# Attention beside an MLP on one core: score banks shared by all, the norm's small steps on GpSimd, and a table of order rules

## The chip, the cores and the metric

The kernel runs on one NeuronCore of a Trainium2 chip. Its engines work side by side, each on an instruction stream of its own, in order: TensorE (PE; its weight loads are PEld), VectorE (DVE), ScalarE (ACT), GpSimd (POOL) and SyncE (SP, which only issues DMAs). Streams wait for each other by semaphores. The metric is the device time of one execution in microseconds (us).

## What is computed

S = 2048 rows of D = 640, H = 32 query heads of width 20 that share one key and one value head, and an MLP of width F = 1536; all data are bfloat16.

```python
xn = (x - mean(x)) / sqrt(var(x) + 1e-5)
q = (xn @ wq) split into 32 heads;  k = xn @ wk;  v = xn @ wv
p = softmax(q @ k.T * 20 ** -0.5)          # per head, 2048 x 2048
A = concat_heads(p @ v) @ wo
B = square(relu(xn @ w1 + b1)) @ w2 + b2
out = x + A + B
```

## The kernel before

**Tiles and blocks.** A score tile has 128 keys by 512 queries of one head, one PSUM bank (PSUM has eight, `ps[:, 0:8]`). A block is one chunk of 512 queries (`QC` = 4) and four heads (`HPG`), so there are 32 blocks (`NBLK`) of 16 key tiles (`KT`) by four heads: 2048 score tiles in all. Each tile goes through one of two ways.

- *By ScalarE.* A step (`make_step`, `build_step`) takes two or three tiles; TensorE writes them with one group of matmuls, each on 20 of its rows (L320, `ps<-qT,kT`), and ScalarE turns them into exponentials with one activation (`make_act`, L864, `PT<-ps`). `PT` is a ring of 20 tiles (`PTR`). When the four heads of a key tile are there, a group of four matmuls on 32 columns each multiplies them with the values (`make_pv`, the PV sum, L320 `ps<-PT,vx`).
- *By VectorE.* Four tiles make a set (`new_set`, `make_dqk`). VectorE makes a linear function of each score whose 16-bit integer is the bit pattern of a coarse exponential (L1066, `D1`, `tmore<-ps`). Three passes over the set (L1084, `P1` to `P3`) add integers to it, and four weighted PV groups (`make_dpv`, `NTERM` = 4) make the sum smooth. A pass runs on GpSimd or on VectorE, chosen by the planned load of the two.

The PV groups of a block add up in one PSUM bank; a row of ones beside the values gives the softmax's denominator. VectorE copies the bank out (`TN`, L957), DMAs and small steps normalise it, and later units multiply it with `wo`.

**Units.** All other TensorE work is cut into units that are put between the steps: the transposes, keys, values and queries, the MLP's first matmul (`FFN`), its second alone (`FP`) or together with the attention's output (`OUT`). Each takes one PSUM bank, which VectorE empties. The last chunk's output is made after the last scores (the tail).

**Who sets the order.** A planner in the kernel's Python builds all streams before anything runs: a loop that holds a planned time for each engine and commits, each time, the operation that can start first, with a priority among those that could start within `EPS` of it. `par(name)` gives the planner's weights. Its table `RULES` can replace weights in single stages, where a stage is 10 us (`STG`) of planned ScalarE time; before, the table is empty. Where TensorE would stand idle too long, the planner puts in groups of four matmuls on zeros (`fill_parts`, L320, `ps<-kT,zeros`). A score group uses TensorE in another shape than the rest, for which the planner counts `SWITCH` at each change.

**Banks before.** `STATIC = True`: ScalarE's steps take banks 0, 1, 2 and banks 3, 4 in turn (`SIDES`), so three tiles and two tiles in turn. VectorE's tiles and the units share the remaining banks 5 to 7, of which the PV sum holds one; at the end of a block the next sum takes another of the three (`bank_for`, `pv_begin`), and `kept` keeps that one free for it. `DV` and the code behind it could let two steps of two tiles follow each other at once, but only without `STATIC`.

**The norm's small steps.** The rows are normalised in 16 parts (`rows(st)`). For most, VectorE makes the statistics (L379 to L381), adds epsilon to the variance (`VE`, L382) and, where the last step is GpSimd's (`POOLXN`), negates the mean (`NM`, L385); GpSimd raises the variance to the power -1/2 (`PW`, L387), and VectorE or GpSimd writes the normalised rows (`XN`, L389). `HOLD` lets loads start when a named operation is planned; that of `b2` hangs on `VE8`. VectorE passes that read and write SBUF alone and GpSimd's passes are marked `lock`, and the planner keeps them apart in its planned time.

The lines of the free choice of banks, which stood in the code before but did not run:

```python
t0 = max(free["PE"], horizon() - par("JIT"))
...
ok = [bk for bk in range(NB) if st_of[bk] is not None and st_of[bk] <= t0 + 0.02]
banks = None
if len(ok) >= 3 + par("R3"):
    ...                            # three adjacent banks of those
if banks is None:
    ...                            # the two adjacent banks that come free first
```

`horizon()` is the planned time at which ScalarE has done all steps so far; `JIT` is 0.8 us and `R3` is 2 by default.

Of the kernel before, what the change touches and what calls it, by code (L numbers as in the profile page):

```python
# [35 lines left out]
def _pl(z):  # L36
# [8 lines left out]
PTR = 20  # L45
NB = 8
PV0 = 7
SHARED = (4, 5, 6)
STATIC = True
SIDES = ((0, 1, 2), (3, 4))  # L50
POOLED = tuple(range(NB))
# [29 lines left out]
DJIT = 9.0  # L81
DV = 9
D1P = 1
RULES = {}
HOOK = None
# [26 lines left out]
DEFAULTS = dict(EVP=EVP, PBIAS=PBIAS, MPRIO=MPRIO, DGAP=DGAP, DLAST=DLAST, DRATE=DRATE, BEHIND=BEHIND, IDLE=IDLE, URG=URG, NOPEN=NOPEN,  # L112
                EPS=0.03, JIT=JIT, R3=R3, STATIC=STATIC, PVA=1, PVD=1, D1P=D1P, PP=4, SQP=2, DQP=3, QKP=0, ND=2, WARM=WARM, KEEP=KEEP, DJIT=DJIT, DV=DV)

# [63 lines left out]
def bass_parallel_sum__grouped_kv_mqa__dense_activation_squared_relu__prompt_kernel(nc, A_x, A_wq, A_wk, A_wv, A_wo, B_x, B_w1, B_b1, B_w2, B_b2, out):  # L178
    es = ExitStack()
    with es:  # L180
# [187 lines left out]
        def rows(st):  # L368

            p = ROWP[st // 4]  # L370
            if st in ACTST:
                k = ACTST.index(st)
                jk = OC[:, 0, :, :].rearrange("p c n -> p (c n)")[:, k * D:(k + 1) * D] if k < 4 else out_sb[:, k - 4, :]
                s1 = op(f"S{st}a", "ACT", 0.72, lambda e: e.activation(out=jk, in_=x_sb[:, st, :], func=AF.Identity, scale=-1.0 / D, accum_out=mv[:, st, 0:1]), [x_op[st]], lat=0.2)  # L374
                ag = op(f"S{st}b", "ACT", 0.9, lambda e: e.activation(out=jk, in_=x_sb[:, st, :], func=AF.Square, bias=mv[:, st, 0:1], accum_out=mv[:, st, 1:2]), [s1], lat=0.25)
                ve = op(f"VE{st}", "DVE", 0.08, lambda e: e.tensor_scalar(out=mv[:, st, 1:2], in0=mv[:, st, 1:2], scalar1=1.0 / D, scalar2=EPS, op0=ALU.mult, op1=ALU.add), [ag], prio=p - 0.1)
                opm = ALU.add
            else:
                s1 = op(f"S{st}a", "DVE", 0.40, lambda e: e.bn_stats(out=stats6[:, st, 0, :], in_=x_sb[:, st, 0:320]), [x_op[st]], prio=p)  # L379
                s2 = op(f"S{st}b", "DVE", 0.40, lambda e: e.bn_stats(out=stats6[:, st, 1, :], in_=x_sb[:, st, 320:640]), [x_op[st]], prio=p)  # L380
                ag = op(f"AG{st}", "DVE", 0.19, lambda e: e.bn_aggr(out=mv[:, st, :], in_=stats6[:, st, :, :].rearrange("p a b -> p (a b)")), [s1, s2], prio=p - 0.1)  # L381
                ve = op(f"VE{st}", "DVE", 0.08, lambda e: e.tensor_scalar(out=mv[:, st, 1:2], in0=mv[:, st, 1:2], scalar1=EPS, scalar2=None, op0=ALU.add), [ag], prio=p - 0.1)  # L382
                opm = ALU.subtract
                if st in POOLXN:
                    s1 = op(f"NM{st}", "DVE", 0.08, lambda e: e.tensor_scalar(out=mv[:, st, 0:1], in0=mv[:, st, 0:1], scalar1=-1.0, scalar2=None, op0=ALU.mult), [ag], prio=p - 0.1)  # L385
                    opm = ALU.add
# [72 lines left out]
        def fill_parts():  # L459
            return [mm(ps[32 * jj:32 * jj + 32, pv_bank[pv_blk[0]], :], zeros32[:, :], kT[:, 0:512], False, False, (0, 32 * jj)) for jj in range(4)]  # L460

        def warm_parts():
            return [lambda e: e.matmul(ps[:, PV0, :], ones_bf[:, :], hT_tmp[:, 0, :], start=True, stop=True)]  # L463

# [337 lines left out]
        def make_step():  # L802
# [7 lines left out]
            t0 = max(free["PE"], horizon() - par("JIT"))  # L810
            keep = kept()
            st_of = {bk: bank_state(bk) if bk != keep else None for bk in range(NB)}
            ok = [bk for bk in range(NB) if st_of[bk] is not None and st_of[bk] <= t0 + 0.02]
# [61 lines left out]

        pv_bank = {0: PV0}
        bank_busy[PV0] = True

        def bank_for(b):

            if b in pv_bank:
                return pv_bank[b]
            can = [(bank_state(bk), -bk) for bk in range(NB) if bank_state(bk) is not None and not (par("STATIC") and bk in HELD)]
            return -min(can)[1] if can else None

        def kept():

            b = pv_blk[0]
            return bank_for(b) if b < NBLK and b not in pv_begun else None

        def pv_begin(b):
            if b not in pv_begun:
                pv_bank[b] = bank_for(b)
                bank_busy[pv_bank[b]] = True
                pv_begun.add(b)

        def make_pv(b, kt):
            first, last = b not in pv_begun, pv_count[b] == KT - 1
            parts, deps = [], []
            bank = bank_for(b)  # L900
            for h in range(HPG):
                o, sl = tile_act[(b, kt, h)]
                deps.append(o)
                parts.append(mm(ps[32 * h:32 * h + 32, bank, :], vx[:, kt, :], PT[:, sl, :], first, last, (0, 32 * h)))
            deps.append(v_op[kt // 4])
            if first:
                deps.append(bank_rel[bank])
            return Op(f"PV{b}_{kt}", "PE", 0.222, parts, deps)

        def make_dpv(s, term):  # L910
# [4 lines left out]
            parts = []  # L915
            bank = bank_for(b)
            for h in range(HPG):
                i = s["order"].index(h)
                parts.append(mm(ps[32 * h:32 * h + 32, bank, :], wgt[:, kt, :], src[:, i * 512:(i + 1) * 512], first, last, (0, 32 * h)))
            deps.append(v_op[kt // 4])  # L920
            if term:
                deps.append(vs_op[kt // 4][term - 1])
            if first:
                deps.append(bank_rel[bank])
            return Op(f"DPV{b}_{kt}_{term}", "PE", 0.2205, parts, deps)
# [14 lines left out]
        def emit_norm(b, lastpv):  # L940
            marg = DMARG if b < NBLK - 3 else DMEND
            qc, g = divmod(b, G)
            a = b % NOR
            pb = pv_bank[b]
            if b >= NBLK - 2:
                Tn, T2 = OR[:, a, :], QCr[:, 0, :]
                tn = op(f"TN{b}", "DVE", 0.63, lambda e: e.transpose(out=Tn, in_=ps[:, pb, :]), [lastpv] + or_users[a], prio=0)
                tn.frees = pb
                rc = op(f"RC{b}", "DVE", 0.155, lambda e: e.reciprocal(out=Tn[:, DH:512:32], in_=Tn[:, DH:512:32]), [tn], prio=0)
# [6 lines left out]
                return  # L956
            tn = op(f"TN{b}", "DVE", 0.60, lambda e: e.tensor_copy(out=OR[:, a, :], in_=ps[:, pb, :]), [lastpv] + or_users[a], prio=0)  # L957
            tn.frees = pb
            tn_op[b] = tn
# [61 lines left out]
        def pool_banks():  # L1021

            keep = kept()
            if par("STATIC"):
                return [bk for bk in POOLED if bk not in HELD and bk != keep and bank_state(bk) is not None]
            fb = [bk for bk in POOLED if bk != keep and bank_state(bk) is not None]
            return fb if len(fb) > par("KEEP") else []
# [72 lines left out]
        def tail_bank():  # L1100
            done = not peek_tiles(1)[0]
            bs = [bk for bk in range(NB) if (bk not in HELD or done) and bank_state(bk) is not None]
            return min(bs, key=lambda bk: (bank_state(bk), bk)) if bs else None

# [67 lines left out]
        while True:  # L1172
# [36 lines left out]
            b = pv_blk[0]  # L1209
            if b < NBLK and (b == 0 or b - 1 in tn_op) and bank_for(b) is not None:  # L1210
                for k, (kind, x) in enumerate(pv_ready[b]):
# [75 lines left out]
            elif kind == "qk":  # L1287
                take_step(ap[1])
                heads = [t[2] for t in ap[1]["tiles"]]
                if len(heads) == 2 and not par("STATIC") and sum(1 for bk in POOLED if bank_state(bk) is not None and bank_state(bk) <= o.start + 0.06) >= par("DV"):  # L1290
                    can = [bk for bk in range(NB - 1) if all(k != kept() and bank_state(k) is not None and bank_state(k) <= o.start + 0.06 for k in (bk, bk + 1))]
                    st_ = build_step(len(steps), [can[0], can[0] + 1], 0.0) if can else None
                    if st_ is not None and len(st_["tiles"]) == 2 and not set(t[2] for t in st_["tiles"]) & set(heads):
                        rd = st_["qk"].ready()
                        if rd is not None and rd <= o.start + 0.06:
                            st_["qk"].dur = 0.005
                            commit(st_["qk"])
                            st_["qk"].lat = 0.425
                            take_step(st_)
                            heads += [t[2] for t in st_["tiles"]]  # L1300
                while len(heads) < HPG:
# [13 lines left out]
            elif kind == "pv":  # L1315
                pv_begin(ap[1])
                pv_of[(ap[1], pv_ready[ap[1]].pop(ap[2])[1])] = o
                finish_pv(ap[1], o)
            elif kind == "dpv":
                pv_begin(ap[1])  # L1320
                s_, term = ap[3], ap[4]
# [128 lines left out]
```

## Time and profile before

| | |
|---|---|
| median of 3 runs (lowest to highest) | 753.14 us (753.05 to 753.17) |
| profiled execution: time, span | 753.17 us, 751.4 us |
| granted TensorE clock | 0.999 |
| busy: TensorE, weight loads, VectorE, ScalarE, GpSimd | 716.6, 241.2, 580.0, 733.5, 292.0 us |
| exp activations (L864) | 640 |
| VectorE's score tiles (L1066) | 448 |
| passes (L1084): VectorE, GpSimd | 199, 137 |
| fills on zeros (`ps<-kT,zeros`) | 936 matmuls |

The span is from the first to the last instruction. Matmuls are pipelined and their ends are modelled, so a busy TensorE is not TensorE at its peak. An instruction's duration can overlap the next one's on the same engine. A releaser behind an arrow is what ended an idle time or a wait. L320 is a helper's line for most matmuls, so that the names of the tiles tell what they are.

### The profile page before, as it was taken

The page shows a single profiled execution, that of the slowest core. Times are in us where ns is not written, and L with a number is a line of the kernel's source. Part 1 is how long each engine was busy: PE and PEld are TensorE (multiplying, and loading weights), DVE is VectorE, ACT ScalarE, POOL GpSimd, SP SyncE. Part 2 cuts the span into 40 slices and gives each one's busy share as a digit, 9 for nine tenths or more (in the row PEclk, how much of TensorE's full clock was granted, in tenths as well). Part 3 has the DMA queues.
Part 4 walks back from the last instruction along what each step waited for, and adds up shares of the span by engine and source line. Part 5 has one row for each costly group of instructions (what it writes and reads, how often), then busy time and mean ns, then how long its engine had stood idle before and what let it go on. Part 6 is the DMA issues. An engine that isn't in the chain of part 4 may idle for free.

```text
span 751.4 us, 23326 instructions
## 1 busy us (share of the span) xinstructions
PE 716.6 (95%) x10359; PEld 241.2 (32%) x10361; DVE 580.0 (77%) x990; ACT 733.5 (98%) x662; POOL 292.0 (39%) x195
## 2 busy tenths in 40 slices
PE   8999998999999999999999999999999999999997
PEld 4432223333222333332222333332222233332223
DVE  7768887786887868969887878778887875777882
ACT  6899999999999999999999999999999999999995
POOL 3714534343553424314135522332434542337452
PEclk9999999999999999999999999999999999999999
DMA  5327232316841111121000111101102111110001
GB/s 188 109 60 195 72 105 66 114 46 141 191 93 28 26 41 45 38 55 27 21 15 16 33 49 51 43 24 35 25 21 90 44 31 56 35 30 20 22 10 37
DMA packets 42017, 44.05 MB, mean 59 GB/s; under 512 B 15540, under 2 KB 32772, under 8 KB 41788
## 3 DMA queue, kind: packets, MB, share of 16 engines
q1 hardware_dynamic: 39132, 36.93, 17.8%
q0 software_dynamic: 2208, 5.25, 3.6%
q8 instruction: 81, 1.33, 0.7%
q10 hardware_dynamic: 576, 0.38, 0.2%
q14 instruction: 20, 0.16, 0.1%
HBM read 28.03 MB, written 14.91 MB: 57 GB/s over the span
## 4 chain that ended last, share of the span: by engine, by line
ACT 94%; PE 4%; DMA 1%; DVE 1%; SPq 0%; issue 0%; DVEq 0%
ACT PT L864 94%; PE ps L320 3%; DMA x_sb<-in_A_x_dram 1%; PE ps L463 0%; PE ps L493 0%; DVE out_sb L1144 0%; PE ps L521 0%; PE ps L449 0%; ACT OC L374 0%; SPq L337 0%; DVE OR L379 0%; DVE kT L507 0%; PE ps L428 0%; SPq L344 0%; ACT xnT L430 0%
## 5 line engine op out<-in xcount | busy, mean ns | idle before, releaser
L864 ACT ACTIVATE PT<-ps 128x1536 bf16<-128x1536 f32 (+1 forms) x640 | 723.8, 1424 | 6.4 <-PE ps L320 6.3
L1066 DVE TENSOR_SCALAR tmore<-ps 128x512 uint16<-128x512 f32 x448 | 299.5, 686 | 112.3 <-PE ps L320 109.7
L320 PE MATMUL ps<-qT,kT 20*128 20x512 bf16 x2048 | 267.9, 384 | 27.7 <-ACT PT L864 24.8
L1084 POOL TENSOR_SCALAR tmore<-tmore 128x2048 uint16<-128x2048 uint16 x81 | 153.4, 1898 | 242.4 <-DVE x_sb L1084 85.8
L1084 POOL TENSOR_SCALAR x_sb<-tmore 128x2048 uint16<-128x2048 uint16 x56 | 106.4, 1902 | 169.6 <-DVE x_sb L1084 114.5
L320 PEld LDWEIGHTS ps<-qT,kT 20*128 20x128 bf16 x2048 | 66.8, 91 | 281.3 <-ACT PT L864 270.9
L320 PE MATMUL ps<-PT,vx 128*32 128x512 bf16 x1600 | 152.9, 387 | 0.6 <-DVE OR L957 0.5
L1084 DVE TENSOR_SCALAR x_sb<-tmore 128x2048 uint16<-128x2048 uint16 x129 | 92.6, 743 | 0.9
L320 PE MATMUL ps<-kT,zeros 128*32 128x512 bf16 x936 | 74.9, 381 | 0.0
L320 PE MATMUL ps<-xnT,w_sb 128*32 128x512 bf16 x960 | 71.0, 382 | 0.0
L320 PE MATMUL ps<-w_sb,big 128*32 128x320 bf16 x1536 | 70.4, 301 | 0.0
L320 PE MATMUL ps<-x_sb,vxs 128*32 128x512 bf16 x740 | 65.9, 382 | 0.2
L320 PEld LDWEIGHTS ps<-PT,vx 128*32 128x32 bf16 x1600 | 39.8, 93 | 74.8 <-issue 68.0
L320 PE MATMUL ps<-tmore,vxs 128*32 128x512 bf16 x604 | 52.3, 381 | 0.0
L1084 DVE TENSOR_SCALAR tmore<-tmore 128x2048 uint16<-128x2048 uint16 x70 | 51.6, 754 | 0.4
L320 PE MATMUL ps<-tmore,vx 128*32 128x512 bf16 x448 | 43.8, 381 | 0.2 <-DVE QCr L565 0.2
L601 DVE TENSOR_SCALAR hT_tmp<-ps,b1col 128x512 bf16<-128x512 f32 x48 | 35.8, 747 | 10.4 <-PE ps L320 10.0
L320 PEld LDWEIGHTS ps<-w_sb,big 128*32 128x32 bf16 x1536 | 34.7, 96 | 25.6 <-issue 16.1
L320 PE MATMUL ps<-xnT,wq_sb 128*32 128x512 bf16 (+1 forms) x480 | 30.8, 355 | 0.0
L320 PE MATMUL ps<-wo_c,OC 128*32 128x320 bf16 x608 | 29.1, 301 | 0.0
L320 PEld LDWEIGHTS ps<-kT,zeros 128*32 128x32 bf16 x936 | 21.7, 95 | 21.7 <-issue 12.6
L320 PEld LDWEIGHTS ps<-xnT,w_sb 128*32 128x32 bf16 x960 | 20.5, 95 | 25.2 <-issue 13.6
(82 smaller groups left out, 300.2 us busy)
## 6 DMA issues: line engine op xcount, KB each, us to landing
xbd<-b2d SPq DMA_DIRECT2D x16, 320.0 KB, 4.4
xbd<-in_A_x_dram POOLq DMA_DIRECT2D x8, 640.0 KB, 6.2
xr<-xbd SPq DMA_DIRECT2D x32, 160.0 KB, 2.4
w_sb<-in_B_w_dram SPq DMA_DIRECT2D x8, 480.0 KB, 5.0
big<-OR SPq DMA_DIRECT2D x71, 40.0 KB
big<-drs SPq DMA_DIRECT2D x71, 40.0 KB
out_dram<-out_sb SPq DMA_DIRECT2D x15, 160.0 KB, 1.8
qT<-QCr SPq DMA_DIRECT2D x108, 20.0 KB
```

The source lines that it names most:

```text
L320: return lambda e: e.matmul(out_, l, r, start=start, stop=stop, tile_position=tp)
L601: o = Op(f"RL{qc}_{f}", "DVE", 0.66, [lambda e: e.tensor_scalar(out=hT_tmp[:, k % 2, :], in0=ps[:, bk, :], scalar1=b1col[:, f:f + 1], scal ...
L864: return Op(f"ACT{st_['j']}", "ACT", 0.05 + 0.4267 * n, [lambda e: e.activation(out=PT[:, s0:s0 + n, :], in_=ps[:, b0:b0 + (n - 1) * db + ...
L1066: d1 = op(f"D1_{n}_{i}", "DVE", 0.60, lambda e: e.tensor_scalar(out=L[:, cs].bitcast(U16), in0=ps[:, bank, :], scalar1=XA, scalar2=XB, op0 ...
L1084: p = op(f"P{j}_{n}", eng, 0.60 if eng == "DVE" else 1.86, lambda e, T=T, j=j, two=two: e.tensor_scalar(out=T.bitcast(U16), in0=L.bitcast( ...
```

## The change

- `STATIC = False`: a step takes its banks from seven (`NB`), 0 to 6, by the rule quoted above; VectorE's tiles and the units take theirs from the same seven (`pool_banks`).
- The PV sum stays in bank 7 (`PVB`). The first PV group of a block waits for the copy `TN` of the block before. `kept`, `bank_for` and `pv_begin` go, and so does the second score step of `DV`.
- In the row parts from the fifth on, `VE` (without ScalarE's statistics) and `NM` are GpSimd's, with other priorities.
- `RULES` gets entries for most of the stages 1 to 69.
- The tail may use bank 7 once the last block's copy is planned.

The core of the diff, with the table of rules cut to a few of its lines:

```diff
 PTR = 20
-NB = 8
-PV0 = 7
+NB = 7
+PVB = 7
 SHARED = (4, 5, 6)
-STATIC = True
-SIDES = ((0, 1, 2), (3, 4))
+STATIC = False
+SIDES = ((0, 1), (2, 3))
 POOLED = tuple(range(NB))
...
 DJIT = 9.0
-DV = 9
-D1P = 1
-RULES = {}
+RULES = {1: {'PVA': 0.95, 'EPS': 0.2, 'DGAP': 0.8},
...
+         3: {'JIT': 0.9, 'R3': 0},
...
+         12: {'R3': 2, 'ND': 1, 'JIT': 1.0, 'MPRIO': 1.1},
...
+         15: {'R3': 1},
...
+         30: {'NOPEN': 3, 'DQP': 2.05, 'EPS': 0.12},
+         38: {'DQP': 2.05, 'PBIAS': 2.5},
...
+         52: {'DGAP': 1.5, 'MPRIO': 0.9, 'BEHIND': 0.5, 'PBIAS': 2.5, 'R3': 1, 'NOPEN': 2, 'D1P': 1, 'DRATE': 1.1, 'DLAST': 3.5, 'EVP': 2, 'EPS': 0.06, 'PP': 4, 'SQP': 0.7, 'URG': 4},
...
+         67: {'R3': 9, 'WARM': 0.78, 'NOPEN': 1, 'URG': 2, 'D1P': 1, 'ND': 2, 'MPRIO': 0.9, 'DQP': 0.95},
...
+         69: {'R3': 0, 'WARM': 0.78, 'NOPEN': 1, 'URG': 2, 'D1P': 0.5, 'ND': 2, 'MPRIO': 0.9, 'DQP': 0.95, 'PBIAS': 1}}
 HOOK = None
 DEFAULTS = dict(EVP=EVP, PBIAS=PBIAS, MPRIO=MPRIO, DGAP=DGAP, DLAST=DLAST, DRATE=DRATE, BEHIND=BEHIND, IDLE=IDLE, URG=URG, NOPEN=NOPEN,
-                EPS=0.03, JIT=JIT, R3=R3, STATIC=STATIC, PVA=1, PVD=1, D1P=D1P, PP=4, SQP=2, DQP=3, QKP=0, ND=2, WARM=WARM, KEEP=KEEP, DJIT=DJIT, DV=DV)
+                EPS=0.03, JIT=JIT, R3=R3, STATIC=STATIC, PVA=1, PVD=1, D1P=1, PP=4, SQP=2, DQP=3, QKP=0, ND=2, WARM=WARM, KEEP=KEEP, DJIT=DJIT)
...
             p = ROWP[st // 4]
+            small, pp = (("DVE", 0.08), p - 0.1) if st < 4 else (("POOL", 0.13), st // 4 - 0.5)
             if st in ACTST:
...
                 ag = op(f"AG{st}", "DVE", 0.19, lambda e: e.bn_aggr(out=mv[:, st, :], in_=stats6[:, st, :, :].rearrange("p a b -> p (a b)")), [s1, s2], prio=p - 0.1)
-                ve = op(f"VE{st}", "DVE", 0.08, lambda e: e.tensor_scalar(out=mv[:, st, 1:2], in0=mv[:, st, 1:2], scalar1=EPS, scalar2=None, op0=ALU.add), [ag], prio=p - 0.1)
+                ve = op(f"VE{st}", *small, lambda e: e.tensor_scalar(out=mv[:, st, 1:2], in0=mv[:, st, 1:2], scalar1=EPS, scalar2=None, op0=ALU.add), [ag], prio=pp)
                 opm = ALU.subtract
                 if st in POOLXN:
-                    s1 = op(f"NM{st}", "DVE", 0.08, lambda e: e.tensor_scalar(out=mv[:, st, 0:1], in0=mv[:, st, 0:1], scalar1=-1.0, scalar2=None, op0=ALU.mult), [ag], prio=p - 0.1)
+                    s1 = op(f"NM{st}", *small, lambda e: e.tensor_scalar(out=mv[:, st, 0:1], in0=mv[:, st, 0:1], scalar1=-1.0, scalar2=None, op0=ALU.mult), [ag], prio=pp)
                     opm = ALU.add
...
         def fill_parts():
-            return [mm(ps[32 * jj:32 * jj + 32, pv_bank[pv_blk[0]], :], zeros32[:, :], kT[:, 0:512], False, False, (0, 32 * jj)) for jj in range(4)]
+            return [mm(ps[32 * jj:32 * jj + 32, PVB, :], zeros32[:, :], kT[:, 0:512], False, False, (0, 32 * jj)) for jj in range(4)]
...
         def warm_parts():
-            return [lambda e: e.matmul(ps[:, PV0, :], ones_bf[:, :], hT_tmp[:, 0, :], start=True, stop=True)]
+            return [lambda e: e.matmul(ps[:, PVB, :], ones_bf[:, :], hT_tmp[:, 0, :], start=True, stop=True)]
...
             t0 = max(free["PE"], horizon() - par("JIT"))
-            keep = kept()
-            st_of = {bk: bank_state(bk) if bk != keep else None for bk in range(NB)}
+            st_of = {bk: bank_state(bk) for bk in range(NB)}
             ok = [bk for bk in range(NB) if st_of[bk] is not None and st_of[bk] <= t0 + 0.02]
...
-        pv_bank = {0: PV0}
-        bank_busy[PV0] = True
-
-        def bank_for(b):
-
-            if b in pv_bank:
-                return pv_bank[b]
-            can = [(bank_state(bk), -bk) for bk in range(NB) if bank_state(bk) is not None and not (par("STATIC") and bk in HELD)]
-            return -min(can)[1] if can else None
-
-        def kept():
-
-            b = pv_blk[0]
-            return bank_for(b) if b < NBLK and b not in pv_begun else None
-
-        def pv_begin(b):
-            if b not in pv_begun:
-                pv_bank[b] = bank_for(b)
-                bank_busy[pv_bank[b]] = True
-                pv_begun.add(b)
-
         def make_pv(b, kt):
...
             parts, deps = [], []
-            bank = bank_for(b)
             for h in range(HPG):
...
                 deps.append(o)
-                parts.append(mm(ps[32 * h:32 * h + 32, bank, :], vx[:, kt, :], PT[:, sl, :], first, last, (0, 32 * h)))
+                parts.append(mm(ps[32 * h:32 * h + 32, PVB, :], vx[:, kt, :], PT[:, sl, :], first, last, (0, 32 * h)))
             deps.append(v_op[kt // 4])
-            if first:
-                deps.append(bank_rel[bank])
+            if first and b > 0:
+                deps.append(tn_op[b - 1])
             return Op(f"PV{b}_{kt}", "PE", 0.222, parts, deps)
...
             parts = []
-            bank = bank_for(b)
             for h in range(HPG):
                 i = s["order"].index(h)
-                parts.append(mm(ps[32 * h:32 * h + 32, bank, :], wgt[:, kt, :], src[:, i * 512:(i + 1) * 512], first, last, (0, 32 * h)))
+                parts.append(mm(ps[32 * h:32 * h + 32, PVB, :], wgt[:, kt, :], src[:, i * 512:(i + 1) * 512], first, last, (0, 32 * h)))
             deps.append(v_op[kt // 4])
...
                 deps.append(vs_op[kt // 4][term - 1])
-            if first:
-                deps.append(bank_rel[bank])
+            if first and b > 0:
+                deps.append(tn_op[b - 1])
             return Op(f"DPV{b}_{kt}_{term}", "PE", 0.2205, parts, deps)
...
             a = b % NOR
-            pb = pv_bank[b]
             if b >= NBLK - 2:
                 Tn, T2 = OR[:, a, :], QCr[:, 0, :]
-                tn = op(f"TN{b}", "DVE", 0.63, lambda e: e.transpose(out=Tn, in_=ps[:, pb, :]), [lastpv] + or_users[a], prio=0)
-                tn.frees = pb
+                tn = op(f"TN{b}", "DVE", 0.63, lambda e: e.transpose(out=Tn, in_=ps[:, PVB, :]), [lastpv] + or_users[a], prio=0)
                 rc = op(f"RC{b}", "DVE", 0.155, lambda e: e.reciprocal(out=Tn[:, DH:512:32], in_=Tn[:, DH:512:32]), [tn], prio=0)
...
                 return
-            tn = op(f"TN{b}", "DVE", 0.60, lambda e: e.tensor_copy(out=OR[:, a, :], in_=ps[:, pb, :]), [lastpv] + or_users[a], prio=0)
-            tn.frees = pb
+            tn = op(f"TN{b}", "DVE", 0.60, lambda e: e.tensor_copy(out=OR[:, a, :], in_=ps[:, PVB, :]), [lastpv] + or_users[a], prio=0)
             tn_op[b] = tn
...
-            keep = kept()
             if par("STATIC"):
-                return [bk for bk in POOLED if bk not in HELD and bk != keep and bank_state(bk) is not None]
-            fb = [bk for bk in POOLED if bk != keep and bank_state(bk) is not None]
+                return [bk for bk in POOLED if bk not in HELD and bank_state(bk) is not None]
+            fb = [bk for bk in POOLED if bank_state(bk) is not None]
             return fb if len(fb) > par("KEEP") else []
...
             bs = [bk for bk in range(NB) if (bk not in HELD or done) and bank_state(bk) is not None]
+            if tn_op.get(NBLK - 1) is not None and tn_op[NBLK - 1].fin is not None and not bank_busy[PVB]:
+                bank_rel[PVB] = bank_rel[PVB] or tn_op[NBLK - 1]
+                bs.append(PVB)
             return min(bs, key=lambda bk: (bank_state(bk), bk)) if bs else None
...
             b = pv_blk[0]
-            if b < NBLK and (b == 0 or b - 1 in tn_op) and bank_for(b) is not None:
+            if b < NBLK and (b == 0 or b - 1 in tn_op):
                 for k, (kind, x) in enumerate(pv_ready[b]):
...
                 heads = [t[2] for t in ap[1]["tiles"]]
-                if len(heads) == 2 and not par("STATIC") and sum(1 for bk in POOLED if bank_state(bk) is not None and bank_state(bk) <= o.start + 0.06) >= par("DV"):
-                    can = [bk for bk in range(NB - 1) if all(k != kept() and bank_state(k) is not None and bank_state(k) <= o.start + 0.06 for k in (bk, bk + 1))]
-                    st_ = build_step(len(steps), [can[0], can[0] + 1], 0.0) if can else None
-                    if st_ is not None and len(st_["tiles"]) == 2 and not set(t[2] for t in st_["tiles"]) & set(heads):
-                        rd = st_["qk"].ready()
-                        if rd is not None and rd <= o.start + 0.06:
-                            st_["qk"].dur = 0.005
-                            commit(st_["qk"])
-                            st_["qk"].lat = 0.425
-                            take_step(st_)
-                            heads += [t[2] for t in st_["tiles"]]
                 while len(heads) < HPG:
...
             elif kind == "pv":
-                pv_begin(ap[1])
+                pv_begun.add(ap[1])
                 pv_of[(ap[1], pv_ready[ap[1]].pop(ap[2])[1])] = o
...
             elif kind == "dpv":
-                pv_begin(ap[1])
+                pv_begun.add(ap[1])
                 s_, term = ap[3], ap[4]
```

## The prediction

> **What bounds the kernel now.** I read the busy shares first, then the chain that ended last, then the groups kept apart by shape, then who waits for whom.
>
> The page's busy line, and the chain that ended last from 41 us on, in order of time (start, length, what):
>
> ```profile
> PE 716.6 (95%) x10359; PEld 241.2 (32%) x10361; DVE 580.0 (77%) x990; ACT 733.5 (98%) x662; POOL 292.0 (39%) x195
> 41.23 698.48 ACT PT L864 x618
> 739.76 6.15 PE ps L320 x137
> ```
>
> 618 of the 640 exp steps of ScalarE stand end to end on the chain. Only less exp time, or a shorter start and tail, can shorten the kernel. The groups by shape (count, busy us, mean ns, idle before):
>
> ```profile
> L864 ACT ACTIVATE PT<-ps 128x1536 bf16<-128x1536 f32 x320 | 522.6, 1633 | 4.9 <-PE ps L320 4.9
> L864 ACT ACTIVATE PT<-ps 128x1024 bf16<-128x1024 f32 x320 | 388.6, 1214 | 1.4 <-PE ps L320 1.4
> L1066 DVE TENSOR_SCALAR tmore<-ps 128x512 uint16<-128x512 f32 x448 | 299.5, 686 | 112.3 <-PE ps L320 109.7
> L320 PE MATMUL ps<-kT,zeros 128*32 128x512 bf16 x936 | 74.9, 381 | 0.0
> ```
>
> ScalarE takes 320 x 3 + 320 x 2 = 1600 score tiles, VectorE 448 (112 sets of four); together the 2048 that exist. The two exp rows add to 911 us, more than ScalarE's whole busy time: durations overlap, so steps must be priced from start to start. Between successive starts in the trace the medians are 1.330 us for a three-tile step and 0.904 us for a two-tile step: 0.426 a tile and 0.052 a step. VectorE is the other consumer of score tiles. Its stretch from 50 to 725 us (PE, weight load, VectorE, ScalarE, GpSimd busy), and its main waits:
>
> ```profile
> 50.00:725.00 675.00, 647.22 (x9300) 211.42 (x9296) 534.93 (x863) 675.00 (x599) 261.25 (x142) 1.00 0.22 56
> PEld ps L320 <- ACT PT L864: 272.2, 630, 1.2
> DVE tmore L1066 <- PE ps L320: 109.7, 174, 2.0
> ```
>
> ScalarE is busy in all 675 us there; VectorE is idle for 675 - 534.93 = 140.1, 108.0 of it before L1066, waiting for TensorE to write a score tile. TensorE runs in order and stands 630 times before ScalarE's next banks; VectorE's tiles queue behind that, and only two banks, with the spare of the three that the PV sum rotates through, are left to them. So the lever is the split of tiles: each that VectorE takes costs ScalarE 0.447 us less (2.234 for five).
>
> **The time as a sum.** The profiled execution took 753.17 us: span 751.4 and 1.8 outside it, equal to the median 753.14 of the runs. The span is 14.7 until the first exp, 320 x 2.234 = 714.9 of steps, 4.4 of four bare gaps before 42 us, 8.9 of small waits inside the chain, and 8.5 after the last exp (742.9).
>
> **Banks and steps.** The change drops the held banks 0-2 and 3-4. A step takes three adjacent banks if at least 3 + R3 of the seven are free in time, else two. By default R3 is 2: five free of seven while ScalarE still holds two or three, so only when VectorE and the units hold at most one or none. R3 is 1 in 17 stages of the table and 0 in seven, where a triple comes easily. I take one step in five as a triple: 2.2 tiles a step against 2.5 now. With two-tile steps ScalarE ties up four banks, and three are left for VectorE and the units.
>
> VectorE should then have its next tile written while it works on the last. If its 108 us of waits for TensorE in this stretch go, it is busy 534.9 + 108 = 643 of 675, 95%. I take 22 more sets (134). Each costs it 4 x 0.607 (start to start) and, with one of three passes on it at 0.65, 3.08 us; 22 cost 68. The stretch itself shrinks by about 22 x 1.79 - 4 = 35. Of 140 us idle 37 stay, 94% busy. The other 44 passes go to GpSimd at 1.9: 84 us, which brings it to 376 of 720. That is cover, as it idles over half of the time.
>
> ```profile
> L1084 DVE TENSOR_SCALAR x_sb<-tmore x129: 652/686/2005, 67.2 to 730.6; 128x2048 uint16<-128x2048 uint16 x129
> L1084 POOL TENSOR_SCALAR x_sb<-tmore x56: 1892/1897/2212, 64.1 to 722.8; 128x2048 uint16<-128x2048 uint16 x56
> 305.57 1.32 DVE L1084 TENSOR_SCALAR x_sb<-tmore 128x2048 uint16<-128x2048 uint16 x1
> ```
>
> These rows (minimum, median, maximum ns) speak against a free move: a VectorE pass, normally 686 ns, reached 2005, and the one at 305.57 lasted 1.32 us beside a GpSimd pass that began at 304.45. In all 14 of 199 passes exceeded 1.2 us, and the excess is 12.7 us. I take the excess in proportion, some 4 us of VectorE's 37 idle. The Trainium skill, SBUF — State Buffer, section "Who interferes with whom", says that GpSimd and a VectorE instruction in a two-port mode exclude each other fully, whoever starts first; if each of the 44 new GpSimd passes blocked VectorE once by 1.3 us (an estimate by that rule and the maximum above), 57 us would be lost and VectorE could take only about ten more sets.
>
> ScalarE then has 1600 - 88 = 1512 tiles: 1512 x 0.426 = 644.1, and 690 steps x 0.052 = 35.9; together 680.0 against 714.9. The smaller steps alone cost 85 x 0.052 = 4.4. The Trainium skill, ScalarE: Activation LUTs, section "What ACT_TABLE_LOAD costs", gives an ACTIVATE 186 ns beside its elements, 93 more for a pointer operand, and an overlap of 93; by that a step's fixed part is an estimated 0.093 to 0.187 us and the smaller steps would cost 8 to 16 us; the two medians above show 0.052, and the measurement decides. All steps in pairs would be 756 and cost 3.4 more; as many triples as now, 4.4 less.
>
> **TensorE.** A score step costs the same for two, three or four matmuls, about 0.32 us to the next start and 0.105 more for the change of shape before it:
>
> ```profile
> 299.98 0.39 PE L320 MATMUL ps<-qT,kT 20*128 20x512 bf16 x2
> 300.30 0.32 PE L320 MATMUL ps<-w_sb,big 128*32 128x320 bf16 x4
> 303.61 0.40 PE L320 MATMUL ps<-qT,kT 20*128 20x512 bf16 x4
> 303.94 0.40 PE L320 MATMUL ps<-PT,vx 128*32 128x512 bf16 x4
> ```
>
> Now: 640 x 0.426 = 273; PV groups of four, 848 x 0.216 = 183; the projections 355 x 0.216 = 77; the output 552 x 0.136 = 75; some 14 beside. That is 622, and 234 fills (936 matmuls on zeros, which need not run) 50 more. After: 690 x 0.426 = 294, PV 378 + 536 groups = 197, the rest alike: 657 of 720, 91%. It fits without fills, but closely; at 756 steps 685, 95%.
>
> **The fixed PV bank.** The sum of a block can start only when VectorE has copied out the last one's: 0.685 us and two handoffs, about 1 us, 31 times. Behind such a wait on TensorE's queue stand the next score steps, and ScalarE waits for those. The planner can put scores or units ahead of it, and 20 PT slots hold nine steps: I take 0. If that cover is gone it is 31 us of TensorE; it can't be a gain, since TensorE waits for that copy only 1.7 us in all now. The second score step that `DV` allows can't run under `STATIC`: its removal costs nothing. SyncE's DMAs stay as many, in another order, with the DMA engines 22% busy: 0.
>
> **The norm's small steps.** Eleven epsilons and seven negations leave VectorE, 18 x 0.064 (start to start) = 1.2 us less, and go to GpSimd, at least 0.1 each (its memset of four columns), at most 0.557 (its power on one column): 2 to 10 us before 31 us, ahead of the powers and norms queued there, and b2's load, released by one of them. A handoff between engines goes away, a queue comes. Exp gaps in this phase are 4.4: I take 0, between -2 and +4. The tail may use the PV bank: 0, between -2 and +2. The table's 69 stages of order weights can't be priced one by one; they and fuller engines act through the inner waits: 12 for 8.9, at least 6 and at most 30.
>
> Sum: 1.8 + 14.7 + 680.0 + 4.4 + 12 + 8.5 = 721.4, **721 us**.
>
> **The rivals.** First, VectorE stays at the 87% of its best 25 us now (21.82 busy from 300 to 325). Then 12 sets fit: 1552 tiles, 709 steps, 661.2 + 36.9 = 698.1, so 739.5. For it: passes that meet on the port, and order rules that push VectorE's tiles aside. Against it: that window had two shared banks. Second, ending slower: TensorE becomes the bound at the score steps. With pairs throughout (756 steps, 685 us of needed work) and no denser packing than now ((622 + 50)/751 = 89%), the time is 685/0.89 = 770. It decides from 0.89 x 753 = 670 us of work, that is (670 - 363)/0.426 = 721 steps, or under 2.10 tiles a step. For it: R3 of 2 makes triples rare, and with every bank shared one late VectorE read can hold the queue. Against it: fills are padding, and its weight loads stand 272 us before ScalarE's banks, time that denser packing can use. Third, tiles stay divided as now and nothing moves: 753, hardly possible with every order changed.
>
> **How the numbers follow.** Forecast 0.57 (704 to 730: with 30 sets VectorE's room is used up, 1480 tiles in 672 steps take 665.4, and 706 us come out, 704 with small waits as now), first rival 0.25 (730 to 748), second 0.16, third 0.02. Range **704 to 748** holds the first two, 0.82. No change means within 0.2% (1.5 us), about what a measurement of this kernel can tell. Faster 0.82, same 0.02, slower 0.16.
>
> **What would show it.** Right: VectorE's L1066 near 536 instead of 448, its waits for scores far under 108, 650 to 720 exp steps mostly of two, fills nearly gone, GpSimd near 370 us busy, ScalarE still without idle. Wrong: L1066 near 448; ScalarE idle before exp for over 30 us released by TensorE; VectorE's passes often near 2 us; or fills as many as now.

## The result, and the profile after

The changed kernel takes 709.93 us (median of three runs, 709.76 to 710.06) against 753.14; the ratio is 0.9426, with a 95% interval of 0.9405 to 0.9448. The profiled execution took 709.76 us, with a span of 708.0. The forecast was 721 in a range of 704 to 748. Where the clock fell in some executions of a kernel below, its time is the median of all of them and its ratio comes from the undisturbed ones alone.

From the page of after, the busy times; from its groups by shape, the exp steps, VectorE's score tiles, the fills and the moved epsilon (count, busy us, mean ns, idle before):

```profile
PE 697.3 (98%) x9787; PEld 218.5 (31%) x9788; DVE 634.3 (90%) x1090; ACT 691.3 (98%) x741; POOL 442.0 (62%) x291
```

```profile
L921 ACT ACTIVATE PT<-ps 128x1024 bf16<-128x1024 f32 x669 | 625.9, 1184 | 3.4 <-PE ps L377 3.2
L921 ACT ACTIVATE PT<-ps 128x1536 bf16<-128x1536 f32 x50 | 79.4, 1622 | 2.1 <-PE ps L377 2.1
L1096 DVE TENSOR_SCALAR tmore<-ps 128x512 uint16<-128x512 f32 x560 | 362.6, 683 | 37.7 <-PE ps L377 33.0
L377 PE MATMUL ps<-kT,zeros 128*32 128x512 bf16 x40 | 3.4, 381 | 0.0
L440 POOL TENSOR_SCALAR mv<-mv 128x1 f32<-128x1 f32 x11 | 2.5, 226 | 4.6 <-DVE nk L501 2.3 <-DVE mv L439 1.8
```

The lines have moved: exp is L921 now, VectorE's score tile L1096, the passes L1114. VectorE has 560 tiles, 140 sets instead of 112, so ScalarE has 669 x 2 + 50 x 3 = 1488 instead of 1600. ScalarE is as full as before (98%); it has less to do. The fills fell from 936 matmuls to 40. The middle stretch and the two waits that carried the prediction:

```profile
50.00:685.00 635.00, 631.70 (x8775) 190.13 (x8779) 588.03 (x975) 634.94 (x675) 405.17 (x219) 1.00 0.23 59
```

```profile
PEld ps L377 <- ACT PT L921: 244.6, 613, 0.8
DVE tmore L1096 <- PE ps L377: 33.0, 84, 1.6
```

VectorE is busy 588.03 of 635 us, 92.6%, where it had 79%, and its wait for a score tile shrank from 109.7 to 33.0 us. The start-to-start medians of the exp steps are unchanged, 0.904 and 1.330 us, so each run below can be taken apart in the same way, from its profiled execution: step time (worked out at 0.426 a tile and 0.052 a step), start (until the first exp), waits (the rest until the end of the last exp) and tail.

| kernel | tiles of ScalarE | steps | step time | start | waits | tail | span |
|---|---|---|---|---|---|---|---|
| before | 1600 | 640 | 714.9 | 14.7 | 13.3 | 8.5 | 751.4 |
| after | 1488 | 719 | 671.3 | 13.7 | 14.0 | 9.0 | 708.0 |
| e1 pairs in before | 1496 | 748 | 676.2 | 15.1 | 14.1 | 15.0 | 720.4 |
| e2 no rules | 1488 | 738 | 672.3 | 15.0 | 15.1 | 17.8 | 720.2 |
| e3 112 sets | 1600 | 760 | 721.1 | 13.8 | 16.2 | 8.5 | 759.6 |
| e4 triples | 1616 | 639 | 721.6 | 15.1 | 26.0 | 8.6 | 771.3 |
| e5 light TensorE | 1492 | 735 | 673.8 | 15.2 | 42.4 | 8.7 | 740.1 |
| e6 held 3 and 2 | 1588 | 635 | 709.5 | 15.9 | 23.4 | 8.8 | 757.5 |
| e7 few GpSimd passes | 1508 | 725 | 680.1 | 15.3 | 16.7 | 8.7 | 720.8 |
| e8 norm on VectorE, no rules | 1492 | 738 | 674.0 | 14.4 | 16.8 | 11.1 | 716.3 |
| e9 as e5, loads spread | 1496 | 737 | 675.6 | 15.1 | 37.1 | 8.5 | 736.3 |
| e10 as e6, loads spread | 1584 | 634 | 707.8 | 16.0 | 16.4 | 8.5 | 748.7 |
| e12 norm on VectorE, rules | 1516 | 725 | 683.5 | 14.3 | 18.2 | 8.8 | 724.8 |
| e13 as e9, more fills | 1496 | 741 | 675.8 | 15.3 | 19.0 | 8.9 | 719.0 |

Of the 43.4 us between the two spans, 43.6 are step time; start, waits and tail cancel. How many sets are opened is decided by the planner before a run, so each expectation below could state it; the runs test what the plan costs on the chip.

### The profile page after: what moved, and what is told of

Its sections match the earlier page's. It is cut to its first block, busy times and chain, and to the rows that moved or that the text cites. A ratio compares the mean times of both kernels' runs of the same rounds, so it can differ in the third digit from the quotient of the medians.

```text
span 708.0 us, 22589 instructions
## 1 busy us (share of the span) xinstructions
PE 697.3 (98%) x9787; PEld 218.5 (31%) x9788; DVE 634.3 (90%) x1090; ACT 691.3 (98%) x741; POOL 442.0 (62%) x291
## 3 DMA queue, kind: packets, MB, share of 16 engines
q8 instruction: 77, 1.26, 0.7%
## 4 chain that ended last, share of the span: by engine, by line
ACT 89%; PE 7%; DVE 1%; POOL 1%; DMA 0%; issue 0%; DVEq 0%
ACT PT L921 89%; PE ps L377 6%; DMA x_sb<-in_A_x_dram 0%; PE ps L551 0%; POOL rstd L445 0%; DVE big L447 0%; PE ps L579 0%; DVE OR L438 0%; DVE xnT L554 0%; DVE out_sb L1177 0%; DVE OR L437 0%; PE ps L521 0%; PE ps L486 0%; POOL big L447 0%; PE ps L507 0%
## 5 line engine op out<-in xcount | busy, mean ns | idle before, releaser
L921 ACT ACTIVATE PT<-ps 128x1024 bf16<-128x1024 f32 (+1 forms) x719 | 681.2, 1214 | 5.5 <-PE ps L377 5.2
L1096 DVE TENSOR_SCALAR tmore<-ps 128x512 uint16<-128x512 f32 x560 | 362.6, 683 | 37.7 <-PE ps L377 33.0
L1114 POOL TENSOR_SCALAR tmore<-tmore 128x2048 uint16<-128x2048 uint16 x107 | 202.3, 1898 | 151.8 <-DVE tmore L1114 40.9
L377 PE MATMUL ps<-qT,kT 20*128 20x512 bf16 x2048 | 283.4, 384 | 2.5 <-ACT PT L921 1.7
L1114 POOL TENSOR_SCALAR x_sb<-tmore 128x2048 uint16<-128x2048 uint16 x108 | 203.8, 1897 | 89.0 <-DVE x_sb L1114 41.5
L377 PE MATMUL ps<-PT,vx 128*32 128x512 bf16 x1488 | 139.3, 386 | 0.9 <-ACT PT L921 0.6
L1114 DVE TENSOR_SCALAR x_sb<-tmore 128x2048 uint16<-128x2048 uint16 x124 | 87.3, 732 | 0.0
L377 PE MATMUL ps<-x_sb,vxs 128*32 128x512 bf16 x928 | 82.5, 382 | 0.0
L377 PE MATMUL ps<-tmore,vxs 128*32 128x512 bf16 x752 | 68.4, 382 | 0.0
L1114 DVE TENSOR_SCALAR tmore<-tmore 128x2048 uint16<-128x2048 uint16 x81 | 60.8, 773 | 0.1
L377 PEld LDWEIGHTS ps<-x_sb,vxs 128*32 128x32 bf16 x928 | 21.4, 95 | 19.4 <-issue 13.2
L377 PEld LDWEIGHTS ps<-xnT,w_sb 128*32 128x32 bf16 x960 | 18.2, 94 | 27.2 <-issue 21.9
L377 PEld LDWEIGHTS ps<-tmore,vxs 128*32 128x32 bf16 x752 | 17.7, 95 | 15.9 <-issue 12.7
```

What stands on the lines that cost most here:

```text
L377: return lambda e: e.matmul(out_, l, r, start=start, stop=stop, tile_position=tp)
L921: return Op(f"ACT{st_['j']}", "ACT", 0.05 + 0.4267 * n, [lambda e: e.activation(out=PT[:, s0:s0 + n, :], in_=ps[:, b0:b0 + (n - 1) * db + ...
L1096: d1 = op(f"D1_{n}_{i}", "DVE", 0.60, lambda e: e.tensor_scalar(out=L[:, cs].bitcast(U16), in0=ps[:, bank, :], scalar1=XA, scalar2=XB, op0 ...
L1114: p = op(f"P{j}_{n}", eng, 0.60 if eng == "DVE" else 1.86, lambda e, T=T, j=j, two=two: e.tensor_scalar(out=T.bitcast(U16), in0=L.bitcast( ...
```

## The experiments

Theory: a step of two tiles leaves VectorE a third bank, VectorE takes more tiles, and this split is the gain. The rivals: the order rules, the free choice of banks by itself, GpSimd's larger share, the norm's move, and TensorE as the bound.

**e1: one edit in the kernel before.**

```diff
-SIDES = ((0, 1, 2), (3, 4))
+SIDES = ((0, 1), (2, 3))
```

> The kernel before with one edit: the held banks are 0-1 and 2-3, so that every ScalarE step has two tiles and banks 4-6 are left to VectorE and the units; no rules, the PV sum still rotates, the norm's steps stay on VectorE. Theory (a third shared bank lets VectorE take more tiles): the plan now has 138 sets, 1496 ScalarE tiles in 748 steps, so 1496 x 0.426 + 748 x 0.052 = 676 of steps and 716 to 724 us in all, VectorE's waits for scores (110 us) mostly gone. Rival A (the order rules carry the gain): 745 or more. Rival B (VectorE stays near 87% busy): about 739.

Measured: 721.98 us, ratio 0.9582 (0.9568 to 0.9596). Its groups and its wait:

```profile
L864 ACT ACTIVATE PT<-ps 128x1024 bf16<-128x1024 f32 x748 | 686.1, 1197 | 6.1 <-PE ps L320 6.1
L1066 DVE TENSOR_SCALAR tmore<-ps 128x512 uint16<-128x512 f32 x552 | 358.8, 682 | 39.8 <-PE ps L320 37.1
```

VectorE's wait for scores is 37.1 us, and it takes 552 tiles. A single line, without rules, without free banks, gives 31 of the 43 us: the step time falls by 38.7, and the tail grows by 6.5. Rivals A and B fall. The line changes two things at once, the size of the steps and the number of banks left over; which of them lets VectorE take more tiles was not tested apart.

**e2: the changed kernel without its table.**

```diff
+RULES = {}
```

> The changed kernel with an empty table of rules: free banks, fixed PV bank, the norm's steps on GpSimd stay. Theory: 140 sets and 738 steps remain in the plan, so 1488 x 0.426 + 738 x 0.052 = 672 of steps, 711 to 724 us in all; the table is worth at most 14 us. Rival A (the rules carry the gain): 735 or more.

Measured: 722.49 us, ratio 0.9602 (0.9579 to 0.9626). The split is that of the changed kernel, 140 sets; the table is worth 12.6 us. Pieces of the chain that ended last, around the last exp, without the table and with it:

```profile
649.84 0.04 issue
649.89 67.57 PE ps L318 x1223
717.45 0.02 issue
717.48 0.49 DVE PT L1118
```

```profile
262.94 24.73 PE ps L377 x359
287.67 0.02 issue
287.69 409.98 ACT PT L921 x428
697.67 0.04 issue
697.72 4.32 PE ps L377 x116
702.04 0.01 issue
702.05 0.89 PE ps L377 x20
```

Without the table TensorE leads the chain for 67.57 us near the end: its units are behind, and 17.8 us of work follow the last exp. With the table it leads for 24.73 us in the middle, while ScalarE stays busy, and 9.0 us follow the last exp. So the table buys 8.8 in the tail, 1.3 in the start, 1.1 in the waits and 1.0 in the steps. TensorE's backlog is real, but it falls on the tail, not on the steps.

**e3: the old split in the new kernel.**

```diff
-            if b >= NBLK or not (b == 0 or b in qt_op):
+            if b >= NBLK or not (b == 0 or b in qt_op) or len(sets) >= min(112, 3.5 * b + 3.5):
```

> The changed kernel with all its parts, but no more than 112 sets may be opened, the number before, spread over the blocks. Theory (only the split of the tiles pays): 1600 tiles in 760 steps, 681.6 + 39.5 = 721 of steps, 755 to 765 us, slower than before by the price of the smaller steps. Rival C (free banks and a better order pay by themselves): 745 or less.

Measured: 761.37 us in a single execution.

```profile
L921 ACT ACTIVATE PT<-ps 128x1024 bf16<-128x1024 f32 x678 | 634.7, 1211 | 5.1 <-PE ps L377 4.9
L1096 DVE TENSOR_SCALAR tmore<-ps 128x512 uint16<-128x512 f32 x448 | 289.4, 682 | 97.1 <-PE ps L377 94.7
```

With everything else in place, the old 448 tiles make it 8 us slower than before: 120 more steps cost 6.2. Rival C falls: free banks, rules and the rest, as they stand, pay nothing without the split. What a table chosen for 112 sets would give was not tried.

**e4: free banks, but triples wherever they fit.**

```diff
-R3 = 2
+R3 = 0
+RULES = {}
```

> The changed kernel with an empty table and R3 = 0: a step takes three banks whenever three adjacent ones are free. The plan has 339 triples of 639 steps and 108 sets. Theory (banks that a step takes are banks that VectorE lacks): 1616 x 0.426 + 639 x 0.052 = 722 of steps, 758 to 770 us. Rival D (fewer, larger steps are cheaper for ScalarE and TensorE, and the split would stay): 735 or less.

Measured: 773.35 us in a single execution, slower than the kernel before and 3 us above the theory's range. Rival D falls. With 339 triples VectorE got 432 tiles and waited 114.9 us for scores:

```profile
L862 ACT ACTIVATE PT<-ps 128x1536 bf16<-128x1536 f32 x339 | 483.1, 1613 | 13.8 <-PE ps L318 13.8
L1037 DVE TENSOR_SCALAR tmore<-ps 128x512 uint16<-128x512 f32 x432 | 286.5, 684 | 116.3 <-PE ps L318 114.9
```

Between e2 and e4 the edit differs only in the triples: fewer steps (639 for 738), and 51 us more. The waits of the exp steps are 26.0 us, 11 more than in e2. The granted clock was 0.5 for 3.4, 6.8 and 3.4 us before the end; e5 shows what such a stretch costs, but not why it came here.

**e6 and e10: the held banks of before in the changed kernel, without the table.** This keeps the fixed PV bank and the norm on GpSimd.

```diff
-STATIC = False
-SIDES = ((0, 1), (2, 3))
+STATIC = True
+SIDES = ((0, 1, 2), (3, 4))
+RULES = {}
```

> The changed kernel with an empty table and the held banks of before, 0-2 and 3-4 in turn: the fixed PV bank and the norm's steps on GpSimd stay. Theory (these parts are worth little beside the banks): 115 sets, 1588 tiles in 635 steps, 676 + 33 = 709 of steps, 744 to 750 us. Rival G (the fixed PV bank costs TensorE 31 us that free banks hid): over 760. Rival H (the norm's move pays by itself): under 740.

Measured: 758.38 us (753.01 to 766.22), ratio 1.0053 (1.0024 to 1.0082): above the theory and below rival G. In its trace the clock was at 0.5 from 190 to 200 us after a 3.6 us stop of TensorE; the mean clock of the ten executions lay between 0.978 and 0.995. e10 spreads the loads that build x + b2:

```diff
-xc=[... f"RL0_{k}" for k in range(4) ...], xb=[f"RL0_{k}" for k in range(6)] + ...
+xc=[... f"RL0_{2 * k + 1}" for k in range(4) ...], xb=[f"RL0_{2 * k}" for k in range(6)] + ...
```

> The kernel of e6 (empty table, held banks 0-2 and 3-4 as before, fixed PV bank, norm's steps on GpSimd) with the same loads spread in the same way. Theory (e6's 758 held some 10 us of the same pile-up, seen at 186 to 200 us with the clock at 0.5; the fixed PV bank and the norm's move are worth little): 116 sets, 1584 tiles in 634 steps, 708 of steps, clock 0.99 or more, 743 to 749. Rival G (the fixed PV bank costs when banks are held): 755 or more with a full clock.

Measured: 750.54 us, ratio 0.9977 (0.9952 to 1.0001), 1.5 above the theory's range, with the clock at 0.995 in its trace; the stop at 186 us is gone. So the fixed PV bank and the norm's move together are worth nothing that can be told from no change, and rivals G and H fall.

**e7: GpSimd keeps its old share of the passes.**

```diff
-eng = "POOL" if tp <= td + par("PBIAS") else "DVE"
+eng = "POOL" if tp <= td + par("PBIAS") and sum(1 for s_ in sets for p_ in s_["passes"] if p_.eng == "POOL") < 137 / 420 * len(tuse) else "DVE"
```

> The changed kernel with its table, but GpSimd gets no larger share of the passes than before (137 of 420, spread over the run). The plan has 135 sets, 133 passes on GpSimd and 272 on VectorE, 725 steps. Theory (VectorE has room for most of the passes too; GpSimd is a convenience): 1508 x 0.426 + 725 x 0.052 = 680, 717 to 723 us, VectorE near 95% busy in the middle. Rival I (VectorE can't carry them, late reads hold TensorE and ScalarE, as the prediction's 87% would have it): 730 or more with ScalarE idle.

Measured: 722.6 us in a single execution. The middle stretch (TensorE, weight load, VectorE, ScalarE, GpSimd):

```profile
50.00:685.00 635.00, 630.28 (x8754) 191.47 (x8746) 594.92 (x998) 632.59 (x667) 250.33 (x136) 1.00 0.23 59
```

VectorE carries 272 passes and 540 tiles at 594.92 of 635, 93.7%, with ScalarE almost without idle. Rival I falls. GpSimd's larger share isn't what makes the gain possible; it is worth five of the 28 sets.

**e8 and e12: the norm's small steps back on VectorE,** without the table and with it.

```diff
-small, pp = (("DVE", 0.08), p - 0.1) if st < 4 else (("POOL", 0.13), st // 4 - 0.5)
+small, pp = ("DVE", 0.08), p - 0.1
```

> The changed kernel with an empty table and the norm's small steps back on VectorE. Against the run with the empty table (first exp at 15.0, exp gaps 3.5 before 42 us). Theory (the move is worth between -2 and +4 us in the start phase): first exp and gaps within 3 us of that run; the plan has 139 sets and 738 steps, 1492 x 0.426 + 738 x 0.052 = 674, 712 to 725 us by the tail. Rival H (the move pays by itself): start phase later by over 4 us and 727 or more.

> The changed kernel with its whole table, only the 18 small norm steps back on VectorE. Theory (the move is worth little, the table fits only the one plan it was chosen for): the plan falls to 133 sets, 1516 tiles in 725 steps, 646 + 38 = 684 of steps, 719 to 728, first exp and its early gaps within 3 us of the changed kernel (13.7 and 4.0). Rival H (the norm's move pays by itself): first exp or the early gaps worse by over 4 us. Rival K (the table carries over): 714 or less.

Measured: e8 719.03 us, ratio 0.9543 (0.9526 to 0.9560), 3.5 below e2; e12 728.23, ratio 0.9663 (0.9636 to 0.9690), 18 above the changed kernel. In both the start differs by under 1 us from its partner, so rival H falls twice. In e12 the 18 small steps change the planner's later choices: seven sets go (12.2 us of step time), and VectorE waits longer for scores again (45.8 us). Rival K falls too: e8 and e12 differ only in the table, and with it the kernel is 9 us slower. The table fits the plan that it was chosen for, and not this one.

**e5, e9 and e13: is TensorE the bound?** Four of the five groups of each FFN unit are left out, without the table.

```diff
-512, dt, dt == DT - 1))) for dt in range(DT)]     # unit_FFN1
+512, 0, True))) for dt in range(1)]
```

> The changed kernel with an empty table, and four of the five matmul groups of each MLP unit (FFN) left out, so that its h is not the reference's: 192 groups or 41 us less for TensorE, nothing less for VectorE. The run with the empty table had 17.8 us after its last exp, led by TensorE. Theory (TensorE is close to full and its leftover makes that tail, but it doesn't set the split): the plan has 139 sets and 735 steps, so the step time stays (1492 x 0.426 + 735 x 0.052 = 674), the tail falls to about 9: 711 to 716. Rival E (TensorE's load sets the split of tiles, the second rival of the prediction): with 41 us freed, 705 or less, exp time falling by 10 us or more. Rival F (the tail is the DMAs' or VectorE's): 719 or more.

Measured: 739.73 us, ratio 0.9808 (0.9744 to 0.9873): less work, and 17 us slower than e2. The tail fell to 8.7 as the theory had it, so rival F falls although its time was reached, and the step time stayed; 42.4 us of waits came. The stop at 180 us among its waits, and, in stretches, the clock (third number from the right) and the busy share of the DMA engines (second):

```profile
DVE R L934 <- DMA R<-drs: 5.9, 1, 5.9
PEld ps L318 <- DVE tmore L1037: 5.5, 1, 5.5
```

```profile
170.00:180.00 10.00, 9.40 (x122) 2.39 (x110) 7.14 (x12) 10.00 (x12) 6.02 (x4) 1.00 1.03 217
180.00:190.00 10.00, 5.43 (x41) 1.10 (x41) 4.92 (x10) 3.81 (x5) 1.29 (x2) 0.54 0.84 186
190.00:200.00 10.00, 10.00 (x74) 1.90 (x74) 5.28 (x10) 6.61 (x7) 0.00 (x0) 0.50 0.13 30
200.00:210.00 10.00, 10.00 (x78) 1.64 (x76) 6.63 (x10) 7.17 (x7) 7.51 (x4) 0.50 0.01 2
```

VectorE waited 5.9 us for the DMA of the denominators, TensorE waited for VectorE, and its clock fell to half. The DMA was probably held up by the loads of x + b2: e2 issued the same transfer at 172.2 us, with the DMA engines 35% busy, and VectorE used it at 178.3 without waiting; here it was issued at 172.1, with the DMA engines full from 160 to 180, and was used at 183.7. At half clock TensorE can't feed ScalarE, which is busy 6.61 and 7.17 of 10 us. e9 spreads those loads as in e10:

> The light-MLP kernel of e5 (four of five groups of each FFN unit left out, empty table), with the loads that build x + b2 in DRAM spread out: they hang on every second FFN unit of the first chunk instead of on each. In e5 one reciprocal's DMA was issued at 172.1 us and VectorE got past it at 183.7, TensorE stood 5.5 us, and its granted clock was 0.5 from 181 to 215 and from 259 to 276 us. Theory (that pile-up of DMAs cost e5 some 27 us, and TensorE's load doesn't set the split): 138 sets, 1496 tiles in 737 steps, 676 of steps, granted clock back to 0.99 or more, 711 to 718. Rival E (TensorE's load sets the split): 705 or less. Rival J (a lighter TensorE loses its clock by itself): clock under 0.98 and 730 or more again.

Measured: 741.66 us, ratio 0.9755 (0.9707 to 0.9803). The theory misses, and rival J's numbers came (clock 0.961 to 0.984). But the edit did not spread the loads enough to test the pile-up: the DMA engines were still 98% busy from 170 to 180, and the stop at 180 us stayed. What speaks for rival J is that the clock fell four more times without such a stop. e13 adds fills and a margin:

```diff
-WARM = 0.72
-DMARG = 4
+WARM = 0.85
+DMARG = 6
```

> The kernel of e9 (four of five groups of each FFN unit left out, loads spread) with two weights changed: fills from a TensorE share of 0.85 instead of 0.72 downwards, which puts 204 groups on zeros for 156, and a margin of 6 us instead of 4 for the DMAs of the softmax's denominators, so that VectorE meets its reciprocal later. In e9 the clock was 0.5 five times, for 44 us in all. Theory (TensorE's load doesn't set the split; the halved clock made e5 and e9 slow): 138 sets, 1496 tiles in 741 steps, 676 of steps, clock 0.99 or more, 710 to 718. Rival E (TensorE's load sets the split): 705 or less. Rival J2 (a TensorE with less needed work can't be kept at its clock by these fills): clock under 0.985 and 725 or more.

Measured: 727.37 us, the median of 721.0, 722.3, 732.4 and 737.0, between theory and rival J2. The two short executions, the profiled one among them, held the clock at 0.999 and 1.0 and lie 3 to 4 us above the theory's range; the two long ones had 0.976 to 0.978. Fills and margin changed together, so their shares are not known. At full clock the step time is again that of e2 (675.8 for 672.3): with 41 us less to do, TensorE wrote no more tiles for VectorE, and rival E falls as far as this planner's splits go. What a planner that counted on the room could do with it wasn't tried. No kernel of these beat the changed one.

## Why the prediction was right

**The mechanism held.** The step "if its 108 us of waits for TensorE in this stretch go" was right in kind; 33 of 110 stayed. ScalarE remained the bound, nearly all steps are pairs, and the gain comes from the split: with it alone 31 us (e1), without it none (e3, e4). The table adds 12.6 on top (e2), most of it by taking back the tail that the split made longer.

**The terms, 721.4 against 709.8.** The term that was mis-sized is the sets: 22 more were forecast, 28 came, 24 tiles or 10.2 us. Part of the fault lay in the passes: one of three new ones was put on VectorE, 22 in all, but it got only 6 of the 84 (199 to 205), and GpSimd 78 (137 to 215). By the prediction's prices 28 sets at 4 x 0.607 and six passes at 0.65 come to 72 us, hardly more than the 68 reckoned for 22. The rest lay in the prices, which were too high: VectorE's busy time rose by only 54.3 us (580.0 to 634.3). In e7, 23 more sets and 73 more passes come to 103 us by them, and it rose by 75.9 (to 655.9). One reason shows in the rows: a score tile took 0.669 us of busy time before (299.5 for 448) and 0.648 after (362.6 for 560), so the old tiles became cheaper too. Steps were more, 719 for 690 (+1.5 us), since triples were 7% and not one in five. Start -1.0, waits -2.4, tail +0.5. Together -11.6.

**Where luck helped.** The tail was kept at 8.5 us with nothing to hold it there. Without the table, which the prediction left unpriced, it was 17.8 (e2) and the whole 722.5 us, close to the forecast because the sets gained about what the tail lost.

**The clash on the port.** VectorE passes over 1.2 us are 11 of 205, for 14 of 199, and the excess is 13.6 us for 12.7, with 78 more passes on GpSimd. The 57 us that the estimate by the Trainium skill's exclusion (SBUF — State Buffer, "Who interferes with whom") would have allowed did not come, since the planner keeps the two kinds apart in time. Where they met, the trace agrees with the rule: all 24 VectorE passes over 0.75 us ran beside a GpSimd pass for over 0.1 us, and of the other 181 only six did, none for more than 0.2 us.

**The first rival,** VectorE staying at 87%, is excluded by 92.6% here and 93.7% in e7. **The second,** TensorE as the bound from 721 steps on, came near by its own count: 719 steps, and needed work of 719 x 0.426 + 932 x 0.216 + 166 = 673 us, 95% of the span. What failed in it is "no denser packing than now". The backlog shows only as the tail in e2. **The third** is excluded by the times.

**The fixed PV bank and the norm's move** were taken at 0. In the changed kernel TensorE waits for the copy of the PV sum 0.2 us in all, and e10 can't be told from no change. The norm's move left the start within 0.6 us (e8, e12); the whole time moved by 3.5 and 18 us, through the planner's later choices. A small step on GpSimd took 0.226 us, within 0.1 to 0.557.

**A gap in the reasoning.** The ledger called the fills work that "need not run". In the changed kernel useful work took their place, so it cost nothing here; in e5 and e9, where TensorE got lighter and had 564 and 536 matmuls on zeros, it spent 51 and 44 us at half its clock. With 728 of them and a larger margin for the DMAs (e13) two of four executions kept it. The prediction had no term for this.

## What to carry to other kernels

When two engines drain the same PSUM banks and one is the bound, count the banks that its steps hold: each step fewer saved 0.052 us here, and steps of two tiles, which leave the other engine a third bank, saved 31 us in all. Test such a belief by one line in the old kernel (e1) and by undoing the supposed cause with all else kept (e3). A table of scheduling weights that was chosen for one plan can cost time on the next: here it was worth 12.6 us on its own plan and cost 9 once 18 small steps had changed the plan. Price it by emptying it, after each edit.

## What the runs showed of the hardware

Taking work from TensorE can slow it. In e9 the granted clock was 0.5 for 13.7, 3.4, 6.8, 6.8 and 13.7 us, always in multiples of 3.4. The first spell began in a pause of 5.4 us between matmul starts, but the other four had no pause over 0.91 us in the 12 us before them. Three stretches, up to and around the second spell and around the third:

```profile
390.00:404.00 14.00, 13.26 (x157) 3.42 (x159) 12.90 (x23) 14.00 (x16) 7.21 (x4) 1.00 0.08 15
400.00:410.00 10.00, 9.36 (x90) 2.16 (x90) 7.13 (x11) 8.93 (x10) 8.29 (x5) 0.83 0.19 45
420.00:430.00 10.00, 9.10 (x84) 2.05 (x80) 9.22 (x14) 8.44 (x9) 6.54 (x4) 0.72 0.13 31
```

The Trainium skill, TensorE: Matmul & The Clock Gate, section "Why this matters for your kernels", advises no idle gaps over about 3 us between bursts of matmuls. The first spell agrees with it; the other four came without such a gap. What set them off the runs don't show: between 30 and 730 us the kernel before has pauses of up to 1.26 us between matmul starts, and e4 has one of 1.74 us at 305 us, and the clock held there. A lighter TensorE isn't needed for it either: with the whole MLP, e4 spent 13.6 us, e6 17.0 and e10 6.8 at half clock before their ends. "Busy" gives no warning, as TensorE shows 13.26 of 14 us up to the second spell.

A late DMA of 8 KB had a long arm: in e5 its landing was 5.9 us late for VectorE, which held TensorE for 5.5 us. The clock fell 1.9 us after the start of TensorE's last matmul, sooner than that advice would have it, and stayed at half for 34 us.
